# The first batch's filter stage in pairs of PSUM banks: 1024-column products and copies, three products on GpSimd, and one input piece on GpSimd's queue

## The chip, the cores and the metric

The kernel runs on one core of one Trainium2 chip. The metric is device time in microseconds (us); lower is better. The kernel before takes 880.41 us, the median of three runs (879.73 to 880.63).

## The reference

Eight sequences of 3008 rows and 256 columns are filtered along the sequence in the frequency domain, and every row of the result then passes through a gated feed-forward layer. Cut to what matters:

```python
X = np.fft.rfft(x, axis=1)                       # x: (8, 3008, 256)
Y = X * (filt_r + 1j * filt_i)[None, :, :]       # filter: (1505, 256)
y = np.fft.irfft(Y, n=3008, axis=1)
t = y.reshape(8 * 3008, 256)
out = (np.maximum(t @ w_gate, 0.0) * (t @ w_val)) @ w_out   # w: (256,1536), (256,1536), (1536,256)
```

## The kernel before

**The work.** A sequence of 3008 = 94 x 32 rows is transformed in two steps. Step A is a 94-point transform as a matmul with the float32 weights `WA`; for batches 0 and 1 it is `a_bank`, 512 columns a time, and every such item shows in the profile as two passes of TensorE (PE). Step B takes 32 points: `fwd(b, i)` makes eight small matmuls into PSUM tiles `psX`, `product` multiplies them by the real (`Ftr`) and the imaginary (`Fti`) filter into `tt` and `uu`, and `inv(b, i)` transforms both back into `psD`, which is copied to SBUF. Each batch has six groups i. Step C (`item_c`, PSUM tile `psY`) is the last transform and gives the rows `yT` of one block of 512; `gv` and `o_part` are the feed-forward layer on 47 such blocks (`psV`, `psG`, `psO`).

**The order.** All order is written out by hand; each engine runs its instructions in the order in which the program issues them, and waits on semaphores. Batch 0 goes first and alone ("first B", the function `first_b`): step A of batch 0 (`a_0`), the transposes `turn_0` on VectorE (DVE), then the six groups of step B. In between stand small things in the hook `amid(i)`: tables for the way back (`make_back_u`), dummy matmuls on a junk tile (`warm`), and items `a_1` of step A of batch 1. After first B the DVE transposes batch 0 once more (`turn_d`), PE works off the rest of the `a_1` items, and the first `item_c` follows; it needs `turn_d`. From there on the feed-forward blocks run without a pause, and steps A and B of batches 1 to 7 are strewn in between them.

**PSUM.** There are eight banks of 512 float32 columns; `bank()` takes the one that has been free longest, and `done()` gives it back. Each `psX`, `psD`, `psA` of first B is one bank.

**First B before.** A group has two `psX` banks (e = 0, 1), so there are 24 products of 512 columns. The list `POOL_U` gives eight of the `uu` products to GpSimd (POOL): ScalarE (ACT) copies `psX` to an SBUF tile `xs` (L427), and POOL multiplies it (L428). The other sixteen run on DVE from PSUM (L430). Group i's products are followed by `inv(0, i-2)`, whose two `psD` banks are copied by ACT (L455), once by DVE.

**Queues.** The filters arrive on POOL's DMA queue; one half of the partitions is then filled from the other by `place_filter` on SP's queue (L256, SBUF to SBUF, `Fti<-Fti`). The first piece of batch 1's input x goes out on SP's queue between those copies (`load_x`, L192), and the rest behind them.

Of the kernel before, what the change touches and what calls it, by code (L numbers as in the profile page):

```python
# [12 lines left out]
FP32 = mybir.dt.float32  # L13
BF16 = mybir.dt.bfloat16
ALU = mybir.AluOpType
# [16 lines left out]
NG = 24  # L32
# [87 lines left out]
def kernel(  # L120
# [10 lines left out]
    nc = tc.nc  # L131
    B, S_, D = x.shape
# [3 lines left out]
    NC2 = 8  # L136
# [9 lines left out]
    consts = ctx.enter_context(tc.tile_pool(name="consts", bufs=1))  # L146
    dram = ctx.enter_context(tc.tile_pool(name="dram", bufs=1, space=bass.MemoryType.DRAM))
    sb = ctx.enter_context(tc.tile_pool(name="sb", bufs=2))
    ps = ctx.enter_context(tc.tile_pool(name="ps", bufs=1, space=bass.MemoryType.PSUM))
    free, held = list(range(8)), {}  # L150

    def bank(name, *shape):

        i = free.pop(0)
        t = ps.tile([128, *shape], FP32, tag=f"bank{i}", bufs=1, name=name)
        held[id(t)] = i, t
        return t

    def done(t):
        free.append(held.pop(id(t))[0])  # L160

    prologue = ExitStack()
    pro = prologue.enter_context(tc.tile_pool(name="pro", bufs=1))

    Abuf = [dram.tile([NROW * N2, D if b > 1 else D // 2], BF16, name=f"Abuf{b}") if b else None for b in range(B)]
    Dbuf = [dram.tile([NROW * N2, D], BF16, name=f"Dbuf{b}") if b else None for b in range(B)]
# [34 lines left out]

    def make_back_t(q):

        psI = [bank("psI", 4, 64) for _ in range(2)]
        for e in range(2):
            for a in range(2):
                for j in range(4):
                    nc.tensor.matmul(psI[e][64 * a:64 * a + 64, j],
                                     F2[64 * e:64 * e + 64, 12 * a + 4 * q + j, :],
                                     perm[64 * e:64 * e + 64], start=True, stop=True,  # L210
                                     tile_position=(64 * e, 64 * a))
        for e in range(2):
            nc.scalar.copy(I2t[:, 8 * q + e:8 * q + 8:2, :], psI[e])
            done(psI[e])

    def make_back_u(q):

        psI = bank("psI", 8, 64)
        nc.tensor.matmul(psI, swap, I2t[:, 8 * q:8 * q + 8, :], start=True, stop=True)
        nc.scalar.copy(I2u[:, 8 * q:8 * q + 8, :], psI)  # L220
        done(psI)

    def place_own():

# [26 lines left out]
    def place_filter(fi, a, half, copy):  # L251

        dst = FILT[fi][1]
        gs = slice(H * half, H * half + H)
        r = a * 64
        copy(dst[r + 32:r + 64, gs, :], dst[r:r + 32, gs, :])  # L256
# [19 lines left out]
        nc.gpsimd.tensor_copy(scr[:tile_.shape[0]], tile_)  # L276


    def a_bank(n2, nn, d0, nd):

        psA = bank("psA", nn, nd)
        xf = XF[n2 // NX2].rearrange("p (n d) -> p n d", d=D)
        n = n2 % NX2
        nc.tensor.matmul(psA, WA, xf[:, n:n + nn, d0:d0 + nd], start=True, stop=True)  # L284
        return psA

    def a_0(n2, nn, d0, nd):

        psA = a_bank(n2, nn, d0, nd)
        dq = D // 4  # L290
        l, q = n2 % NC2, slice(d0 // dq, (d0 + nd) // dq)
        dst = AS0.rearrange("p q (l c) d -> p l c q d", c=N2 // NC2)[:, l:l + nn, n2 // NC2, q, :]
        nc.scalar.copy(dst, psA.rearrange("p n (q d) -> p n q d", d=dq))
        done(psA)

    def a_1(p, s, h):

        psA = a_bank(NC2 * p + 4 * s, 4, h * D // 2, D // 2)
        if h and len(AS1) == 1:
            for _ in range(2):  # L300
                t = sb.tile([128, NC2 * D], BF16, tag="asb", bufs=3, name="asb")
                AS1.append(t.rearrange("p (l c d) -> p l c d", l=NC2, c=N2 // NC2))
        ts = AS1[1:] if h else AS1[:1]
        w = D // 2 // len(ts)
        for i, t in enumerate(ts):
            nc.scalar.copy(t[:, 4 * s:4 * s + 4, p, :], psA[:, :, i * w:(i + 1) * w])
        done(psA)

    def turn_a(dst, src):
# [86 lines left out]
                              _ap(Abuf[b], (48 * (rr % 2) + 24 * (rr // 2)) * N2 * D,  # L396
                                  [[D, 32], [N2 * D, 24], [1, D]]))

    POOL_U = ((0, 1), (1, 0), (1, 1), (2, 0), (2, 1), (3, 1), (4, 0), (5, 0))
    ats = {}  # L400

    psXs, tus, dsbs, left = {}, {}, {}, {}
# [13 lines left out]
                                     ats[b][64 * e:64 * e + 64, j, :] if b > 1 else ats[b][64 * e:64 * e + 64, :, j, :],  # L416
                                     start=True, stop=True, tile_position=(64 * e, 64 * a))

    def product(b, i, e, k, pool=False):

        psX = psXs[b, i, e]
        pool_, bufs = (fs, 4) if b else (pro, 6)
        p = pool_.tile([128, 2, D], BF16, tag=("tt", "uu")[k], bufs=bufs, name=("tt", "uu")[k])
        filt = (Ftr, Fti)[k][:, 4 * i + e:4 * i + 4:2, :]
        if pool:
            xs = pro.tile([128, 2, D], FP32, tag="xs", bufs=3)
            nc.scalar.copy(xs, psX)  # L427
            nc.gpsimd.tensor_tensor(p, xs, filt, op=ALU.mult)  # L428
        else:
            nc.vector.tensor_tensor(p, psX, filt, op=ALU.mult)  # L430
        tus[b, i, e, k] = p
        left[b, i, e] -= 1
        if not left[b, i, e]:
            done(psX)

    def inv(b, i):

        if b and i in CUTS:
            dsbs[b] = i, sb.tile([128, 2, 4, D], BF16, tag="dsb", bufs=3, name="dsb")
        psD = [bank("psD", 2, D) for a in range(2)]  # L440
        for m in range(2):
            for k in range(2):
                for a in range(2):
                    for e in range(2):
                        nc.tensor.matmul(psD[a][64 * e:64 * e + 64, m],  # L445
                                         (I2t, I2u)[k][64 * a:64 * a + 64, 4 * i + 2 * m + e, :],
                                         tus[b, i, e, k][64 * a:64 * a + 64, m],
                                         start=(k == 0), stop=(k == 1),
                                         tile_position=(64 * a, 64 * e))
        if b:  # L450
            i0, dsb = dsbs[b]
            o = 2 * (i - i0)
        for a in range(2):
            copy = nc.vector.tensor_copy if (b, i, a) == (0, 5, 0) else nc.scalar.copy
            copy(dsb[:, a, o:o + 2, :] if b else DS0[:, 12 * a + 2 * i:12 * a + 2 * i + 2, :], psD[a])  # L455
            done(psD[a])
        if b and i + 1 in CUTS:
            for q in range(4):
                nc.sync.dma_start(_ap(Dbuf[b], (64 * (q // 2) + q % 2) * NG * D + 2 * i0 * D,
                                      [[2 * NG * D, 32], [NG // 2 * D, 2], [1, (o + 2) * D]]),  # L460
                                  dsb[32 * q:32 * q + 32, :, :o + 2, :])

    def first_b(amid):

        for i in range(6):
            fwd(0, i)
            on_pool = [(i, e) in POOL_U for e in range(2)]
            seq = {(0, 0): ((0, 0), (0, 1), (1, 0), (1, 1)), (0, 1): ((1, 1), (0, 0), (0, 1), (1, 0)),
                   (1, 0): ((0, 1), (1, 0), (1, 1), (0, 0)), (1, 1): ((0, 0), (1, 1), (0, 1), (1, 0))}
            for e, k in seq[tuple(map(int, on_pool))]:  # L470
                product(0, i, e, k, pool=k == 1 and on_pool[e])
            if i > 1:
                inv(0, i - 2)
            amid(i)
        inv(0, 4)
        amid(6)
        inv(0, 5)

    dCs = {(0, z): dCb[:, 8 * z:8 * z + 8, :] for z in range(NZ)}

# [96 lines left out]

    def warm(n, cols=512):

        psJ = bank("psJ", 512)  # L580
        for i in range(n):
            nc.tensor.matmul(psJ[:, :cols], junk[:, 0:128], junk[:, :cols], start=True, stop=True)
        done(psJ)

    q = NX2 * D // 4
    both, sp = (nc.sync, nc.scalar), (nc.sync,)
# [19 lines left out]

    warm(18, 256)
    new_at(0)
    for n2, h in ((0, 0), (0, 1), (4, 0), (4, 1)):
        a_0(n2, 4, h * D // 2, D // 2)  # L610
    for i, (p, dq) in enumerate(((1, 0), (1, 1), (2, 0), (2, 1), (3, 0), (3, 1), (1, 2), (2, 2), (3, 2),
                                 (1, 3), (2, 3), (3, 3))):
        a_0(NC2 * p, NC2, dq * D // 4, D // 4)
        if p == 3:
            turn_0(dq)
        if i > 9:
            make_back_t(i - 10)
    make_back_t(2)
    for i in range(3):
        warm(2)  # L620
    place_filter(1, 0, 0, nc.gpsimd.tensor_copy)
    for fi, a, half in ((0, 0, 0), (0, 1, 0), (1, 1, 0), (0, 0, 1), (0, 1, 1)):
        place_filter(fi, a, half, nc.sync.dma_start)
    load_x(1, sp, ((0, 0, 2 * q),))
    for a in range(2):
        place_filter(1, a, 1, nc.sync.dma_start)
    load_x(1, sp, ((0, 2 * q, 4 * q), (1, 0, 2 * q), (1, 2 * q, 4 * q)))
    items = iter([(p, s, h) for p, h in ((0, 0), (1, 0), (2, 0), (0, 1), (3, 0), (1, 1), (2, 1), (3, 1))
                  for s in range(2)])

    def amid(i):
        if i < 3:
            make_back_u(i)
            warm(3)
        else:
            a_1(*next(items))
        if i == 3:
            place_nyq()
            place_own()

    first_b(amid)
    load_vg(0, DFF // 2)
    load_vg(DFF // 2, DFF)
    load_o()
# [92 lines left out]
```

## Time and profile before

| | |
|---|---|
| Median of the runs | 880.41 us (879.73 to 880.63) |
| The profiled execution | 880.49 us, with a span of 878.4 us |
| Busy in the span | PE 99%, DVE 66%, ACT 57%, POOL 41% |
| Transfers | 102.85 MB, 117 GB/s in the mean |

The profile is one execution. "Span" runs from the first to the last instruction; 2.09 us of the time lie outside it. Times within it are counted from its start. In the lists by time, a row gives start, duration, engine, line of the code, operation, output and inputs, how many instructions were merged, and in brackets the idle time before them with what ended it. PEld are the weight loads of TensorE, which run beside its matmuls.

### The profile page before, as it was taken

To read this page: it belongs to the slowest core of one execution; us is meant where nothing else is said; L and a number is where in the kernel's file an instruction comes from. 1 tells how busy PE (TensorE), PEld (TensorE's weight loads), DVE (VectorE), ACT (ScalarE), POOL (GpSimd) and SP (SyncE) were. 2 spreads that over 40 slices of the span, in tenths; PEclk is the share of its full clock that TensorE was granted. 3 is DMA by queue.
4 is the path that set the end of the run, shared out by engine and by line. 5 is a ranking of instruction groups with operands and counts; after the bars stand their busy time and mean duration, and the time that the engine had idled before them with its cause. 6 is when DMAs were issued, how large, how long until landed. Compare 5 with 4: busy or idle time off the path is not lost.

```text
span 878.4 us, 19202 instructions
## 1 busy us (share of the span) xinstructions
PE 868.5 (99%) x7184; PEld 507.4 (58%) x7184; DVE 576.5 (66%) x863; ACT 500.7 (57%) x905; POOL 364.3 (41%) x367
## 2 busy tenths in 40 slices
PE   8899999999999999999999999999999999999998
PEld 3445655666555665556655665556655656666665
DVE  4787766667666776567665777657766577655553
ACT  4865655565555656555655565555565555555553
POOL 7718940166901688017870287603884000000001
PEclk9999999999999999999999999999999999999999
DMA  9996454634754347634475344663445512421111
GB/s 251 239 179 110 133 140 106 128 93 102 187 120 101 105 109 181 132 92 101 119 190 114 83 117 126 166 126 88 124 134 141 119 40 69 98 60 36 38 32 53
DMA packets 107075, 102.85 MB, mean 117 GB/s; under 512 B 24216, under 2 KB 92344, under 8 KB 106215
## 3 DMA queue, kind: packets, MB, share of 16 engines
q1 hardware_dynamic: 83974, 74.45, 34.7%
q0 software_dynamic: 22608, 26.41, 13.0%
q8 instruction: 56, 0.92, 0.5%
q10 hardware_dynamic: 400, 0.79, 0.3%
q14 instruction: 37, 0.29, 0.1%
HBM read 58.16 MB, written 45.88 MB: 118 GB/s over the span
## 4 chain that ended last, share of the span: by engine, by line
PE 95%; DMA 3%; POOL 1%; DVE 1%; ACT 0%; issue 0%; SPq 0%; DVEq 0%; POOLq 0%
PE psV L526 29%; PE psG L526 28%; PE psO L547 27%; PE psF L377 3%; PE psY L509 2%; PE psD L445 2%; PE psX L414 2%; PE psA L284 2%; DMA Fti<-Fti 1%; DMA XF<-in_x_dram 1%; DMA Fti<-in_filt_i_dram 1%; POOL out_dram L571 0%; DMA out_dram<-XF 0%; DVE uu L430 0%; DVE prod L531 0%
## 5 line engine op out<-in xcount | busy, mean ns | idle before, releaser
L531 DVE SCALAR_TENSOR_TENSOR prod<-psG,vsb 128x512 bf16<-128x512 f32 x564 | 388.4, 689 | 256.2 <-ACT vsb L529 250.1
L529 ACT CAST vsb<-psV 128x512 bf16<-128x512 f32 x564 | 331.9, 589 | 262.8 <-PE psV L526 171.1
L526 PE MATMUL psV<-yT,WvT 128*128 128x512 bf16 x1128 | 336.7, 379 | 0.6 <-DVE yT L517 0.6
L547 PE MATMUL psO<-WoT,prod 128*128 128x256 bf16 x2256 | 336.5, 273 | 0.0
L526 PE MATMUL psG<-yT,WgT 128*128 128x512 bf16 x1128 | 335.3, 379 | 0.0
L547 PEld LDWEIGHTS <-prod 128*128 128x128 bf16 x2256 | 220.7, 98 | 143.4
L526 PEld LDWEIGHTS <-WgT 128*128 128x128 bf16 x1128 | 110.0, 98 | 134.5 <-issue 1.5
L276 POOL CAST scr<-prod 128x8 f32<-128x8 bf16 x24 | 4.5, 189 | 284.5 <-DVE prod L531 284.5
L526 PEld LDWEIGHTS <-WvT 128*128 128x128 bf16 x1128 | 98.3, 98 | 41.4 <-issue 30.2
L571 POOL DMA_DIRECT2D out_dram<-osb x5 | 2.7, 535 | 200.1 <-ACT osb L560 200.0
L560 ACT COPY osb<-psO 128x512 f32<-128x512 f32 x92 | 53.9, 586 | 25.9 <-PE psO L547 23.8
L430 DVE TENSOR_TENSOR tt<-psX,Ftr 128x512 bf16<-128x512 f32 x96 | 64.8, 680 | 0.9 <-PE psX L414 0.5
L430 DVE TENSOR_TENSOR uu<-psX,Fti 128x512 bf16<-128x512 f32 x88 | 59.8, 680 | 1.9 <-DMA Fti<-Fti 1.9
L363 POOL TENSOR_TENSOR fold<-XF 128x1024 f32<-128x1024 f32 x24 | 57.6, 2401 | 3.7 <-DMA XF<-in_x_dram 3.0
L350 POOL DMA_DIRECT2D XF<-in_x_dram x96 | 56.7, 596 | 3.7 <-PE psY L509 1.5
L364 POOL TENSOR_TENSOR XF<-XF 128x1024 f32<-128x1024 f32 x24 | 56.4, 2350 | 1.9
L455 ACT CAST dsb<-psD 128x512 bf16<-128x512 f32 x84 | 45.1, 589 | 11.0 <-PE psD L445 11.0
L384 DVE CAST asb<-psF 128x512 bf16<-128x512 f32 x48 | 30.9, 686 | 17.8 <-PE psF L377 17.8
L384 ACT CAST asb<-psF 128x512 bf16<-128x512 f32 x48 | 25.8, 589 | 29.0 <-PE psF L377 29.0
L515 ACT CAST yT<-psY 128x512 bf16<-128x512 f32 x47 | 27.5, 586 | 23.1 <-PE psY L509 23.0
L509 PE MATMUL psY<-M,dCb 96*128 96x94 bf16 (+19 forms) x604 | 37.5, 198 | 0.0
L509 PEld LDWEIGHTS <-dCb 96*128 96x128 bf16 (+1 forms) x604 | 34.5, 97 | 3.3 <-issue 0.8
(69 smaller groups left out, 472.2 us busy)
## 6 DMA issues: line engine op xcount, KB each, us to landing
XF<-in_x_dram POOLq DMA_DIRECT2D x48, 256.0 KB, 6.2
Dbuf<-dsb SPq DMA_DIRECT2D x84, 128.0 KB
dCb<-Dbuf SPq DMA_DIRECT2D x56, 192.0 KB
XF<-in_x_dram POOLq DMA_DIRECT2D x96, 96.0 KB, 2.7
Abuf<-asb SPq DMA_DIRECT2D x96, 96.0 KB
at<-Abuf SPq DMA_DIRECT2D x24, 384.0 KB
out_dram<-osb SPq DMA_DIRECT2D x69, 94.0 KB
XF<-in_x_dram SPq DMA_DIRECT2D x20, 256.0 KB
```

Of the source, the lines that this page charges most:

```text
L350: nc.gpsimd.dma_start(xp[r:r + 24, 0:4:2, :], _ap(x, (b * N1 * N2 + o) * D, [[N2 * D, 24], [47 * N2 * D, 2], [1, 512]]))
L363: tt(t, xp[:, 0:2], xp[:, 2:4], op=ALU.add)
L364: tt(xp[:, 2:4], xp[:, 0:2], xp[:, 2:4], op=ALU.subtract)
L384: copy(asf[:, :, q, :], banks[q])
L430: nc.vector.tensor_tensor(p, psX, filt, op=ALU.mult)
L455: copy(dsb[:, a, o:o + 2, :] if b else DS0[:, 12 * a + 2 * i:12 * a + 2 * i + 2, :], psD[a])
L509: nc.tensor.matmul(psY[:, o:o + w], dCs[b, n2 // 8][:, n2 % 8, h * 128:(h + 1) * 128], M1[:, 1, n1:n1 + w] if b == 0 else M1[:NROW, 0, n1: ...
L526: nc.tensor.matmul(pt[:, :W], w[:, h, ft * 128:(ft + 1) * 128], yt[:, h, :], start=(h == 0), stop=(h == 1))
L529: nc.scalar.copy(vsb, psV[:, :W])
L531: nc.vector.scalar_tensor_tensor(prod, in0=psG[:, :W], scalar=0.0, in1=vsb, op0=ALU.max, op1=ALU.mult)
L547: nc.tensor.matmul(psO[:, t % 2], prods[ft][:, t * 128:(t + 1) * 128], WoT[:, ft, :], start=(ft == 0), stop=(ft == NFT - 1))
L560: copy(osb[:, t0 % 2:t % 2 + 1], psO[:, t0 % 2:t % 2 + 1])
```

## The change

First B uses four pairs of banks from a pool of its own, `ps0`, with fixed parts: pairs 0 and 1 are `psX`, pair 2 is `psD`, pair 3 is `psA` of batch 1 and the junk. A product, an `xs` copy and a `psD` copy then cover 1024 columns in one instruction. `POOL_U` goes: POOL has the `uu` product of groups 1, 2 and 4. The three `make_back_u` stand ahead of first B, and `place_own` ahead of it too; of the 512-column junk matmuls, six stand ahead of first B as before, and four instead of three in each of the groups 0, 1 and 2. `amid` of groups 3, 4 and 5 has two `a_1` items each, with one pair and one set of copies; before, groups 3, 4, 5 and one more call had one each. The first x piece of batch 1 goes out on POOL's queue, and the last two filter copies on SP's queue move up ahead of the other pieces. After first B the pool is closed and the eight single banks are used as before.

```diff
+    def pair(i, name):
+        return ps0.tile([128, 2, 512], FP32, tag=f"pair{i}", bufs=1, name=name)
...
     def make_back_t(q):
-        psI = [bank("psI", 4, 64) for _ in range(2)]
+        psI = pair(3, "psI").rearrange("p e (j n) -> p e j n", n=64)
...
-        for e in range(2):
-            nc.scalar.copy(I2t[:, 8 * q + e:8 * q + 8:2, :], psI[e])
-            done(psI[e])
+        nc.scalar.copy(I2t[:, 8 * q:8 * q + 8, :].rearrange("p (j e) n -> p e j n", e=2), psI[:, :, 0:4])
...
+    def a_1_pair(p, h):
+        psA = pair(3, "psA")
+        for s in range(2):
+            a_mm(psA[:, s], NC2 * p + 4 * s, 4, h * D // 2, D // 2)
+        out_1(psA.rearrange("p s (l d) -> p (s l) d", d=D // 2), p, 0, NC2, h)
...
+    def first_fwd(i):
+        psX = pair(i % 2, "psX").rearrange("p e (m d) -> p e m d", m=2)
...
+    def first_product(i, k, psX, pool):
+        p = pro.tile([128, 2, 2, D], BF16, tag=("tt", "uu")[k], bufs=3, name=("tt", "uu")[k])
+        filt = FILT[k][1][:, 4 * i:4 * i + 4, :].rearrange("p (m e) d -> p e m d", e=2)
+        if pool:
+            xs = pro.tile([128, 2, 2, D], FP32, tag="xs", bufs=2, name="xs")
+            nc.scalar.copy(xs, psX)
+            nc.gpsimd.tensor_tensor(p, xs, filt, op=ALU.mult)
+        else:
+            nc.vector.tensor_tensor(p, psX, filt, op=ALU.mult)
...
+    def first_inv(i):
+        psD = pair(2, "psD").rearrange("p a (m d) -> p a m d", m=2)
+        inv_mm([psD[:, a] for a in range(2)], 0, i)
+        dst = DS0[:, 0:NG, :].rearrange("p (a o) d -> p a o d", a=2)[:, :, 2 * i:2 * i + 2, :]
+        if i < 5:
+            nc.scalar.copy(dst, psD)
+        else:
+            nc.vector.tensor_copy(dst[:, 0], psD[:, 0])
+            nc.scalar.copy(dst[:, 1], psD[:, 1])
...
         for i in range(6):
-            fwd(0, i)
...
+            psX = first_fwd(i)
+            pool = i in (1, 2, 4)
+            for k in (1, 0) if pool else (0, 1):
+                first_product(i, k, psX, pool and k == 1)
             if i > 1:
-                inv(0, i - 2)
+                first_inv(i - 2)
             amid(i)
-        inv(0, 4)
-        amid(6)
-        inv(0, 5)
+        first_inv(4)
+        first_inv(5)
...
     for i in range(3):
-        warm(2)
+        make_back_u(i)
+    warm(6)
     place_filter(1, 0, 0, nc.gpsimd.tensor_copy)
-    for fi, a, half in ((0, 0, 0), (0, 1, 0), (1, 1, 0), (0, 0, 1), (0, 1, 1)):
+    for fi, a, half in ((0, 0, 0), (0, 1, 0), (1, 1, 0), (0, 0, 1), (0, 1, 1), (1, 0, 1), (1, 1, 1)):
         place_filter(fi, a, half, nc.sync.dma_start)
-    load_x(1, sp, ((0, 0, 2 * q),))
-    for a in range(2):
-        place_filter(1, a, 1, nc.sync.dma_start)
+    load_x(1, (nc.gpsimd,), ((0, 0, 2 * q),))
     load_x(1, sp, ((0, 2 * q, 4 * q), (1, 0, 2 * q), (1, 2 * q, 4 * q)))
+    place_own()
...
         if i < 3:
-            make_back_u(i)
-            warm(3)
+            warm(4)
         else:
-            a_1(*next(items))
-        if i == 3:
+            a_1_pair(*((0, 0), (0, 1), (1, 0))[i - 3])
+        if i == 2:
             place_nyq()
-            place_own()
 
     first_b(amid)
+    front.close()
+    ps = ctx.enter_context(tc.tile_pool(name="ps", bufs=1, space=bass.MemoryType.PSUM))
+    items = [(p, s, h) for p, h in ((2, 0), (3, 0), (1, 1), (2, 1), (3, 1)) for s in range(2)]
```

In the built program, before and after hold the same instructions from the first `item_c` on; the order on each engine differs only ahead of it. Of `a_1` items, two-pass each, nine are left between the last `inv` and the first `item_c` after the change, and eleven before it.

## The prediction

> **What bounds the kernel now.** I read the busy time by stretches first, to see in which part time can be won at all.
>
> ```profile
> 0.00:40.00 40.00, 34.93 (x270) 15.82 (x271) 22.63 (x26) 25.63 (x49) 30.04 (x45) 1.00 0.92 251
> 50.00:860.00 810.00, 809.35 (x6779) 477.10 (x6778) 539.18 (x824) 462.33 (x828) 328.07 (x312) 1.00 0.46 111
> ```
>
> The first pair of numbers is the stretch and its length, the next is PE's busy time. From 50 us on PE stands still for 0.65 us of 810: that part is work, and the change doesn't touch it. So the whole question is when the first feed-forward matmul (`psV`) starts; what comes behind it moves along one for one. The chain of waits, in order of time (start, duration, what), shows what sets that moment:
>
> ```profile
> 28.09 4.53 DMA Fti<-Fti
> ...
> 32.74 0.70 DVE uu L430
> ...
> 37.61 1.06 PE psA L284 x2
> 38.66 0.56 PE psD L445 x16
> 39.23 9.64 PE psA L284 x22
> 48.86 0.47 PE psY L509 x12
> 49.33 0.95 PE psA L284 x2
> 50.28 0.43 PE psV L526 x2
> ```
>
> The last filter copy lands at 32.65 and holds up a `uu`; then DVE and PE pass the work on closely, and from 39.2 PE runs eleven `a_1` items (x22 passes, 9.64 / 11 = 0.87 each) up to `psY`. `turn_d` is hidden there. The instructions by time:
>
> ```profile
> 36.21 1.09 ACT L455 CAST AS<-psD 128x512 bf16<-128x512 f32 x2
> 37.54 1.13 PE L284 MATMUL psA<-XF,WA 128*128 128x512 f32 x2
> 40.06 7.35 DVE L311 STREAM_TRANSPOSE dCb<-AS 128x2048 f32<-128x2048 f32 x2
> 49.37 0.69 DVE L517 CAST yT<-psY 128x512 bf16<-128x512 f32 x1 [1.96 <-PE psY L509]
> 50.12 0.59 PE L526 MATMUL psV<-yT,WvT 128*128 128x512 bf16 x2
> ```
>
> `turn_d` ends at 47.41, 1.3 us before `psY`. `psV` starts at 50.12: the number to beat. Prices come from the groups by shape (count, then busy and mean ns):
>
> ```profile
> L455 ACT CAST AS<-psD 128x512 bf16<-128x512 f32 x11 | 6.2, 630 | 0.1
> L306 ACT CAST asb<-psA 128x256 bf16<-128x256 f32 x14 | 4.5, 375 | 1.6 <-PE psA L284 1.6
> L428 POOL TENSOR_TENSOR uu<-xs,Fti 128x512 bf16<-128x512 f32 x8 | 9.1, 1153 | 3.3 <-ACT xs L427 2.3 <-DMA Fti<-Fti 0.8
> L430 DVE TENSOR_TENSOR uu<-psX,Fti 128x512 bf16<-128x512 f32 x4 | 2.7, 682 | 1.9 <-DMA Fti<-Fti 1.9
> ```
>
> **Prices of the wide forms** (estimates; no row shows them). ACT undisturbed takes 0.58 for 512 columns and 0.375 for 256, so 0.8 ns a column and 0.99 for 1024; in a row each takes 0.10 less. Its ends are 0.90 and twice 0.58 = 1.16; I take the slope. DVE follows the next every 0.60; at 1024 I take 1.13 (duration 1.21; ends 1.18 and 1.36). POOL's `fold` takes 1.27 at 512 and 2.41 at 1024, so 1.155 becomes 2.25.
>
> **What is shed.** DVE: sixteen products x 0.60 = 9.6 become nine x 1.13 = 10.2, so nothing is won. POOL: 9.2 become 6.8. ACT: eight `xs` and eleven `psD` copies x 0.48 = 9.1 become three and five x 0.89 and one x 0.58 = 7.7. Two `a_1` items, 1.7, move from behind first B into it. The last two filter copies on SP's queue no longer wait behind three x issues (24.47 to 27.26): they go out at about 25.4 and 26.0 instead of 27.36 and 28.09, and at 4.5 land by 30.6. DVE's 1.89 stall on them goes. But what is late next is another thing, below.
>
> **POOL's queue.** It now issues three x pieces (0.5 to 0.6 each) between 23.87 and 25.6 and the two `place_own` copies (0.29 each) by 26.3. POOL was idle there until 26.22 and now gets its first `xs` at 28.5: nothing is queued behind it in need, and it costs nothing. `uu` of group 2 ends at 33.0, `inv(2)` wants it at 33.8; `uu` of 4 ends at 37.7, `inv(4)` comes at 39.7. The weight loads behind it go out at 37.7, as before (37.61).
>
> **What is added: hand-overs.** Before, eight banks rotate, so PE may run ahead of the copies. After, `psD` is one pair and `psA` one pair, so each `inv` waits for the copy of the last one, and each `a_1` pair for its own predecessor's; PE is in order, so `fwd` of the next group is queued behind. The waits in the built program say the same: each `psD` and `psA` group waits for ACT. I lay this out step by step, an instruction starting when its engine is free and its inputs are there, 0.05 for a hand-over. The same reckoning on the kernel before gives 50.07 for `psV`, against 50.12 measured.
>
> - The tables: `make_back_t` has one pair, so each of the three waits for a copy (0.58). Third copy 23.67 to 24.25, third `make_back_u` at 24.30, then six junk matmuls x 0.216. `fwd(0)` starts at 25.81; before, it started at 25.01 when the transpose was done.
> - `tt(0)` 26.30, `uu(0)` 27.43 to 28.64. `fwd(2)` needs pair 0: 28.69. `xs(2)` 29.18 to 30.17, behind it on ACT the copy of `psD(0)`, to 31.06.
> - `inv(1)` 31.11; `a_1` pair: 0.20 for its weights and 4 x 0.43, 31.55 to 33.52; copy (0.99) to 34.56.
> - Second pair 34.61 to 36.58; two copies of 512 (1.06) to 37.69. Third pair 37.74 to 39.72; copy to 40.76. In between ACT copies `psD`; behind the third it is `psD(4)`, to 41.64.
> - `inv(5)` 41.69 to 42.33. Its DVE half to 43.06, and the ACT half waits for DVE in the built program (before, both ran at once, 39.26 and 39.30): to 43.69. Closing the pool makes the first single-bank `a_1` wait for that copy.
> - Nine `a_1` items: 0.20 + 9 x 0.857 = 7.9, 43.74 to 51.65. `turn_d` (7.35) runs 43.74 to 51.08 and stays hidden by 0.6. `psY` 51.65, 0.43, the last `a_1` 1.06, `psV` at 53.14.
>
> DVE, freed from the filter, stands idle for `xs(4)` until 35.50 instead: 1.9, as long as the stall that went. Sum: 53.14 - 50.07 = 3.07 later. In other words: PE reaches the single `a_1` items at 38.96 in the same reckoning before and at 43.74 after, 4.78 later, and the two items already done give back 1.71. On this execution's 880.49 (span 878.4 and 2.09 around it) that is 883.56; the median is 0.08 lower, so 883.5. Five wide ACT copies and two wide products lie on this chain: their ends give -0.5 and +1.15.
>
> **A clock that could drop.** After, between 40.3 and 43.7 PE is busy for about 0.5 us; before, the thinnest such stretch, 22.0 to 25.4, has 2.30 busy of 3.4, and the passes behind it keep their 0.43. So no row shows what so little work does. That there is a slower pace the start shows: eighteen 256-column matmuls in 4.02 us, 0.22 each, the time that 512 columns take later, while the granted clock reads 1.00 there too. The Trainium skill, "TensorE: Matmul & The Clock Gate", speaks against the change here: its section "A second HAM failure mode: psum-queue depth-cycling" tells of a PE that idles a little at every round of its banks and swings between half and full rate, and "What's actually happening" puts the idle window at about 3.4 us. By the first, the single `a_1` items would start slowly; by the second, two gaps of 1.6 us each stay below the limit unless they count as one.
>
> **The rivals.**
> - *Half pace from 43.7.* The start ran slowly from 1.1 to at least 4.95 and at full pace by 7.87, so for some 5 us. The same again, with the nine items on it, does 2.5 us of work in 5: 883.5 + 2.5 = 886.0. For it: the thin stretch; against it: neither gap is over 1.6, and one of 1.1 before left no trace.
> - *The x piece lands late.* POOL's 256 KB loads took 10.2 us in the median in the first 80 us; the third, issued at 25.1, would land at 35.3, and the first `a_1` pair, due at 31.55, holds PE for 3.8: 887.3. Against it: that median is from loads of 2 KB runs in a crowd; here the rows are 8 KB, and 0.8 MB at the 250 GB/s of this stretch need 3 us.
> - *Faster: DVE, not the hand-overs, sets first B.* From 26.3 nine products x 1.13 and the two waits for `xs` of 0.5 end at 37.5, `inv(5)` at 38.0, the split copy and `turn_d` at 46.8, `psV` at 48.3: 878.7 or a little less. For it: this bounds it before, after 32.7. It needs the chain from `inv(1)` to the first single `a_1` (31.1 to 43.7, 12.6) to take under 9.5 to break even; its four `a_1` and copy steps alone are 9.1, so almost no wait could be left.
> - *Partly so*: hand-overs and copies shorter than priced by over 1.4 in all: within the bound, about 881.5.
>
> That the change doesn't do what it says is out: the built program has the 1024-column products, three on POOL, and the filter copies ahead.
>
> **How the numbers follow.** A measurement of this kernel can tell about 0.2% (1.8 us, 878.6 to 882.2) from no change. Chances: 0.66 for the forecast (slower), 0.10 for half pace and 0.08 for the late x piece (both slower), 0.10 for the partial case (same), 0.06 for the faster rival. Slower 0.84, same 0.10, faster 0.06. The range goes from 881.6, the partial case, to 886.2, the half-pace case; the late piece and the faster rival are left out.
>
> **What would show it.** Right: `fwd(0)` near 25.8; no wait for `Fti<-Fti` on DVE, but 1 to 2 us for `xs`; `a_1` pairs each waiting for an ACT copy; a PE gap of 1.6 before `inv(5)` and one before the first single `a_1`; `psV` near 53.1; after it the same 0.65 us of stalls. Wrong: `psV` before 51.5, or `psX` and `psD` groups that wait for DVE alone; passes of `psA` at over 0.5 (half pace); PE waiting for XF (x late); 1024-column copies that aren't near 0.99.

## The result, and the profile after

The changed kernel takes 885.58 us in the median of four runs (884.99 to 886.98), the kernel before beside it 880.52 (four runs): 1.0061 times the time, interval 1.0043 to 1.0078. It is slower by 5.06; the forecast was 883.5, slower by 3.07. The profiled run took 886.10, with a span of 884.1.

The chain of waits of the changed kernel, in order of time (start, duration, what), cut to first B's hand-overs:

```profile
32.34 0.63 PE psD L444 x16
32.97 1.93 PE psA L284 x4
...
34.92 1.02 ACT dCb L304
...
35.98 2.00 PE psA L284 x4
...
38.00 1.08 ACT asb L304 x2
...
39.13 2.00 PE psA L284 x4
...
41.15 1.01 ACT dCb L304
42.16 0.92 ACT AS L498
...
43.13 0.66 PE psD L444 x16
...
43.80 0.70 DVE AS L500
...
44.53 0.59 ACT AS L501
...
45.17 9.69 PE psA L284 x18
54.86 0.47 PE psY L546 x12
```

Before, the chain from 37.61 on was PE alone; now PE and ACT take turns, one pair at a time, as forecast. But the last step but one has a size that nobody put down for it: nine items as x18 passes take 9.69, and before, eleven items as x22 passes took 9.64. The rows by time of the same trace (in brackets the idle time before the row, and what ended it):

```profile
36.88 1.22 DVE L488 TENSOR_TENSOR tt<-psX,Ftr 128x1024 bf16<-128x1024 f32 x1 [1.99 <-ACT xs L485]
43.13 0.30 PE L444 MATMUL psD<-tt,I2t 64*64 64x256 bf16 x4 [1.45 <-ACT AS L498]
45.15 7.26 DVE L321 STREAM_TRANSPOSE dCb<-AS 128x2048 f32<-128x2048 f32 x2 [0.65 <-ACT AS L501]
45.17 9.69 PE L284 MATMUL psA<-XF,WA 128*128 128x512 f32 x18 [1.41 <-ACT AS L501]
56.11 0.59 PE L563 MATMUL psV<-yT,WvT 128*128 128x512 bf16 x2
```

The two gaps of the forecast, 1.45 ahead of `inv(5)` and 1.41 ahead of the first single `a_1`, are there, and DVE waits for `xs` rather than for the filter. `psV` comes at 56.11 instead of 50.12. What the 9.69 is shows in the busy time by stretches (stretch, length, busy PE, PEld, DVE, ACT and POOL with counts, then the granted clock, the DMA share and GB/s):

```profile
41.80:45.20 3.40, 0.66 (x17) 0.39 (x16) 0.74 (x2) 1.86 (x3) 2.19 (x4) 1.00 1.14 195
45.86:49.27 3.41, 3.41 (x6) 1.36 (x5) 3.41 (x2) 1.17 (x2) 0.00 (x0) 0.50 1.15 204
49.27:52.68 3.41, 3.41 (x9) 1.49 (x9) 3.14 (x1) 2.18 (x6) 0.00 (x0) 1.00 1.44 196
```

Between 41.8 and 45.2 PE is busy for 0.66 of 3.40; soon after, its granted clock halves. The trace records when the clock changes: to half at 45.86 and back at 49.27, 3.41 later. At half pace that loses 1.70, and at full pace the same x18 take 7.96 to 7.99 (below). The Trainium skill, "TensorE: Matmul & The Clock Gate", section "What's actually happening", speaks of a free-running window of some 3.4 us; the 3.41 agrees with it, and no gap here is near that long by itself.

Starts within an execution move by about a microsecond with the first loads, so traces are compared from the start of the last `a_0` item (20.96 before, 22.07 after) to `psV`: 29.16 before, 34.04 after. The times of the two profiled runs differ by 5.61: 4.88 in this distance, 1.11 ahead of it, and -0.38 behind (880.49 - 50.12 = 830.37 before, 886.10 - 56.11 = 829.99 after). The last `a_0` of eleven further profiles started anywhere from 19.69 to 22.69, so the 1.11 of one pair of profiles is no finding. Behind `psV` nothing has moved.

### The profile page after: what moved, and what is told of

Read it like the earlier page. It is cut to its first block, busy times and chain, and to the rows that moved or that the text cites. A ratio compares the mean times of both kernels' runs of the same rounds, so it can differ in the third digit from the quotient of the medians.

```text
span 884.1 us, 19047 instructions
## 1 busy us (share of the span) xinstructions
PE 863.4 (98%) x7066; PEld 508.3 (57%) x7187; DVE 577.5 (65%) x856; ACT 499.2 (56%) x888; POOL 363.2 (41%) x365
## 4 chain that ended last, share of the span: by engine, by line
PE 93%; ACT 2%; DVE 2%; issue 1%; DMA 1%; POOL 0%; DVEq 0%
PE psG L563 28%; PE psO L584 27%; PE psV L563 26%; PE psA L284 3%; PE psF L387 3%; PE psD L444 2%; PE psY L546 2%; PE psX L423 2%; DVE prod L568 2%; ACT vsb L566 1%; DMA XF<-in_x_dram 1%; POOL out_dram L608 0%; ACT dCb L304 0%; ACT AS L498 0%; DMA out_dram<-XF 0%
## 5 line engine op out<-in xcount | busy, mean ns | idle before, releaser
L563 PE MATMUL psG<-yT,WgT 128*128 128x512 bf16 x1107 | 330.8, 379 | 5.1
L563 PE MATMUL psV<-yT,WvT 128*128 128x512 bf16 x1030 | 315.5, 380 | 0.9 <-DVE yT L554 0.6
L432 DVE TENSOR_TENSOR tt<-psX,Ftr 128x512 bf16<-128x512 f32 x84 | 57.2, 681 | 0.0
L432 DVE TENSOR_TENSOR uu<-psX,Fti 128x512 bf16<-128x512 f32 x84 | 57.2, 681 | 0.0
L284 PE MATMUL psA<-XF,WA 128*128 128x512 f32 x64 | 31.5, 634 | 5.5 <-issue 1.7
```

Source lines behind the costliest of these rows:

```text
L432: nc.vector.tensor_tensor(p, psX, FILT[k][1][:, 4 * i + e:4 * i + 4:2, :], op=ALU.mult)
L563: nc.tensor.matmul(pt[:, :W], w[:, h, ft * 128:(ft + 1) * 128], yt[:, h, :], start=(h == 0), stop=(h == 1))
```

## The experiments

Two theories were set against each other: the hand-overs of single pairs make all of the loss, or they make some 3.2 and the halved clock the rest. A third question was what the queues do.

**Fill the gaps (fill).** Junk matmuls in the two gaps, into the pair that `a_1` uses:

```diff
         first_inv(4)
+        warm(4)
         first_inv(5)
+        warm(6)
```

> The changed kernel with four junk matmuls between the last two inv and six behind the last one, in PE's two gaps of 1.4 us; nothing waits for their result. Theory (hand-overs cost 3.1, and the thin stretch from 41.7 to 45.2 halves PE's clock for 3.4 us, 1.7 lost): the granted clock stays 1.00 between 40 and 50 us, the 18 passes of the single a_1 items take 7.8 instead of 9.69, and the time falls by 1.7 to about 883.9, still 3.2 above the kernel before. Rival (the passes are slow because transfers or turn_d run beside them): they stay near 9.7, and the time near 885.6.

Measured: 884.10 (five runs), the kernel before 880.36 in the same comparison, ratio 1.0044 (1.0027 to 1.0062). In its profile the clock stayed at 1.00 between 40 and 50 us and the x18 took 7.96, with `turn_d` and the transfers still beside them, so these are not what slows the passes. One of the five runs (887.51) has a mean clock of 0.998. But another wait had come in, the first `a_1` pair on its input:

```profile
31.91 1.52 PE L284 MATMUL psA<-XF,WA 128*128 128x512 f32 x3 [0.94 <-DMA XF<-in_x_dram]
```

This execution's front had come 2.0 earlier (last `a_0` at 20.08). The x pieces on POOL's queue had gone out only 0.94 earlier (23.26 instead of 24.20), and their median time to landing was 6.9 instead of 5.8. So the run was repeated with the queues as before the change.

**The queues put back (undoq), and both (fillq).** undoq is the change without its queue part; fillq is fill and undoq together.

```diff
-    for fi, a, half in (..., (1, 0, 1), (1, 1, 1)):
+    for fi, a, half in (...):
         place_filter(fi, a, half, nc.sync.dma_start)
-    load_x(1, (nc.gpsimd,), ((0, 0, 2 * q),))
+    load_x(1, sp, ((0, 0, 2 * q),))
+    for a in range(2):
+        place_filter(1, a, 1, nc.sync.dma_start)
```

> The changed kernel with the queue part undone: the first x piece on SP's queue between the filter copies, as before. Theory: the pairs' chain runs beside either order, so the time stays within 0.7 of the changed kernel; the Fti copy lands near 32.7 and uu of group 3 waits some tenths for it. Rival (the x piece on POOL's queue holds PE): 1 or more faster.

> The changed kernel with the junk matmuls in PE's two gaps, as before, and with the first x piece back on SP's queue, since with those matmuls alone PE then waited 0.9 for that piece. Theory (hand-overs 3.1, clock 1.7): from the start of the last a_0 item to the first psV 32.3, where the changed kernel has 34.0 and the kernel before 29.2; clock 1.00 in nearly all runs; time 1.7 below the changed kernel, about 3.3 above the kernel before. Rival (the clock has no part; 34.0 is the hand-overs' own): 34.0 and 5 above.

Measured: undoq 886.29 (884.39 to 886.67, four runs), a second look at the changed kernel beside it 885.09; distance 34.03 in both. The queues are worth nothing inside the change: DVE waits 0.31 for the filter copy again, and 1.58 instead of 1.99 for `xs`. fillq took 884.66 (five runs) against 880.14: 1.0049 (1.0037 to 1.0062). Its rows by time and by stretches:

```profile
44.95 7.96 PE L284 MATMUL psA<-XF,WA 128*128 128x512 f32 x18
54.16 0.59 PE L565 MATMUL psV<-yT,WvT 128*128 128x512 bf16 x2
```

```profile
40.00:50.00 10.00, 9.36 (x56) 4.00 (x55) 6.27 (x4) 5.34 (x9) 3.59 (x6) 1.00 1.12 175
```

The distance is 32.44 as expected: with every hand-over still in place, 1.60 of the 4.88 is gone, and on this path only the junk and, with it, the clock differ from undoq. By distance fillq should lie 3.28 above the kernel before; its median lies 4.5 above. That 1.2 is not explained: behind `psV` its profiled run has 831.17, 0.8 more than before, but other profiles scatter there from 829.86 to 831.66.

**The same kernel again (after_again).**

> The changed kernel itself, beside the others on one chip, since runs of one kernel scatter by about 1 us. Both theories: about 885.5, 5 above the kernel before; in the profile the granted clock falls to about half for some 3 us behind the last inv.

Measured: 885.09 (884.06 to 888.24, six runs), ratio 1.0057 (1.0040 to 1.0074). Of the ten runs of the changed kernel in the two comparisons, nine have a mean clock of 0.995 to 0.998 and one has 1.000 (884.65). Half pace for 3.4 of 884 us is a mean of 0.998, so the drop seems frequent but not certain. The mean also counts a half pace at the end of the kernel, where PE has nothing left to do (in fill's profile from 879.59 on). A mean of 0.998 comes in the kernel before too (7 of 60 runs, none lower), so a single such run of another kernel proves nothing; half of the changed kernel's ten runs lie lower.

**All products on DVE (alldve).** The three wide products of POOL and their copies go.

```diff
-            pool = i in (1, 2, 4)
+            pool = False
```

> The changed kernel with all twelve products on DVE, none on POOL, and no xs copies. Theory (PE and ACT hand-overs set the stage, not POOL or DVE): DVE takes 3.4 more and ACT 2.7 less, both beside the chain; the time stays within 1 of the changed kernel. Rival (three of twelve on POOL is what costs, through xs copies ahead of psD copies on ACT): 1.5 or more faster. Rival (DVE is the bound): 2 or more slower.

Measured: 886.28 (884.88 to 886.51, four runs), ratio 1.0062 (1.0046 to 1.0078). Its profiled execution (884.88, clock 1.000) is the case that the forecast had in mind, since it has both gaps and no drop:

```profile
42.73 0.30 PE L444 MATMUL psD<-tt,I2t 64*64 64x256 bf16 x4 [1.46 <-ACT AS L498]
44.77 7.99 PE L284 MATMUL psA<-XF,WA 128*128 128x512 f32 x18 [1.41 <-ACT AS L501]
54.01 0.59 PE L563 MATMUL psV<-yT,WvT 128*128 128x512 bf16 x2
```

```profile
41.40:44.80 3.40, 0.66 (x17) 0.39 (x16) 0.74 (x2) 1.86 (x3) 0.00 (x0) 1.00 1.19 205
```

A stretch with the same 0.66 busy of 3.40 ended without a drop here; its other three runs have clocks of 0.995 to 0.998 and took 1.2 to 1.6 more. So the hand-overs alone make a distance of 32.38, 3.22 more than before, and POOL's share of the products is worth nothing either way: the same distance came out of fillq with three products on POOL.

**Single banks for `a_1` in first B (asplit); the last `inv` into the free `psX` pairs (inv5).** asplit replaces pair 3 by two banks with a copy of each; inv5 takes `psD` of the last group from pairs 0 and 1 and copies both halves on DVE.

```diff
-        psA = pair(3, "psA")
         for s in range(2):
-            a_mm(psA[:, s], ...)
-        out_1(psA..., p, 0, NC2, h)
+            psA = hbank(s, "psA")
+            out_1(a_mm(psA, ...), p, 4 * s, 4, h)
```

```diff
+        if i == 5:
+            psDs = [pair(a, "psD")[:, 0]... for a in range(2)]
...
-            nc.scalar.copy(dst[:, 1], psD[:, 1])
+            nc.vector.tensor_copy(dst[:, 1], psDs[1])
```

> The changed kernel with psA of first B in two single banks instead of one pair, and a 512-column copy behind each item (the tables' psI and the junk use the same two banks). Theory (the hand-over at the one psA pair is on the path): the first copy runs beside the second item, so each of the three a_1 steps gets about 0.5 shorter; the first psV comes 1.6 earlier, at about 54.5 where the profile of the changed kernel has 56.1, and the time falls to about 884.0, with the clock drop still there. Rival (x or filter transfers hold the stage): no change, 885.6.

> The changed kernel with the last inv writing to the two psX pairs, which are free by then, instead of waiting for psD, and both of its copies on DVE. Theory: the gap of 1.45 ahead of the last inv goes, the copies take 1.3 instead of 1.37, and turn_d and the single a_1 items start 1.6 earlier: 884.0 if the clock still drops, about 882.3 if it doesn't, since only one thin gap is left. Rival (the stage ends with what DVE or the transfers allow): no change, 885.6.

Measured, each against 880.36: asplit 883.32 (ten runs, 1.0025, 1.0014 to 1.0036), inv5 883.05 (ten runs, 1.0026, 1.0011 to 1.0042). Rows by time of asplit, then of inv5:

```profile
41.77 0.30 PE L447 MATMUL psD<-tt,I2t 64*64 64x256 bf16 x4 [1.11 <-ACT AS L501]
43.81 7.99 PE L288 MATMUL psA<-XF,WA 128*128 128x512 f32 x18 [1.41 <-ACT AS L504]
```

```profile
43.51 7.96 PE L284 MATMUL psA<-XF,WA 128*128 128x512 f32 x18 [1.43 <-ACT AS L502]
```

asplit's distance is 31.53 and holds 0.55 of waiting for the x piece; without that 30.98, so the waits of the `a_1` pairs were 1.4 of the 3.22. inv5's is 30.68: its gap ahead of `inv(5)` is gone, which is 1.7 of the 3.22, and the gap of 1.43 that the closing of the pool makes remains. In both profiles the clock stayed at 1.00, where asplit's expectation had the drop. The thinnest 3.40 us of first B's end have 0.87 us of PE work in asplit and 1.97 in inv5. Three of asplit's ten runs and two of inv5's have a mean clock of 0.998 or less, and they are the slowest of each.

**Both, and the pool kept open (best1), with four junk matmuls fewer (best2).** The single `a_1` items run on pairs 2, 0 and 1 of `ps0`, and the pool is closed ahead of the first `item_c`. shortwarm is the changed kernel with the last edit alone.

```diff
     first_b(amid)
-    front.close()
-    ps = ctx.enter_context(tc.tile_pool(name="ps", ...))
...
         if (p, s, h) == (3, 0, 1):
+            front.close()
+            ps = ctx.enter_context(tc.tile_pool(name="ps", ...))
```

```diff
-    warm(6)
+    warm(2)
```

> The changed kernel, still with 1024-column products and psD copies, but without its hand-overs: psA of first B in two single banks with a copy each, the last inv on the freed psX pairs with both copies on DVE, and the nine single a_1 items on banks of the same pool, so that they needn't wait for its closing. Theory (hand-overs and the clock that drops in their gaps are the whole loss): psV comes 2.8 earlier than in the reckoning for the changed kernel, at about the same distance from the last a_0 item as in the kernel before (29.2) and not 34.0; clock 1.00; time about 880.8. Rival (a rest of the loss lies in the wide instructions, in POOL's share or in the queue): 882.5 or more.

> The version without hand-overs (two single psA banks, last inv on the psX pairs, single a_1 items on the open pool) with two junk matmuls instead of six ahead of first B. Theory: 0.86 off its 29.8, so 29.0 from the last a_0 item to psV, level with the 29.2 of the kernel before; time 880.4 to 881.0. If the wide instructions were worth anything by themselves: below 880.

> The changed kernel with two junk matmuls instead of six behind the make_back_u. Theory (they are on the path, as the tables hold PE until 24.5 in the reckoning and the transpose ends at 25.0): fwd of group 0 starts 0.86 earlier, and so does psV if the clock does the same as in the changed kernel: 33.2 from the last a_0 item instead of 34.0; time about 884.7. Rival (the later chain swallows it): 34.0, and 885.5.

Measured: best1 881.72 (twelve runs) against 880.56, 1.0013 (1.0005 to 1.0022); best2 881.35 (eleven runs) against 880.14, 1.0013 (1.0004 to 1.0021); shortwarm 885.69 (four runs), 1.0064 (1.0049 to 1.0080). best1's rows by time:

```profile
42.35 7.99 PE L288 MATMUL psA<-XF,WA 128*128 128x512 f32 x18 [0.68 <-ACT AS L511]
51.12 0.62 PE L559 MATMUL psY<-M,dCb 128*128 128x94 bf16 x12 [0.78 <-ACT asb L308]
52.53 0.59 PE L576 MATMUL psV<-yT,WvT 128*128 128x512 bf16 x2
```

The distance falls to 29.84, 0.68 above before, and the wait for the closing of the pool now stands ahead of `psY` (0.78). The parts do not add up: asplit's 1.4 and inv5's 1.7 are 3.1, while best1, which has both edits and this new wait, is 2.54 below alldve's 32.38. In twelve runs the mean clock was never under 0.999; the thinnest 3.40 us ahead of its nine items have 2.72 us of work. Giving the pairs their freedom back undoes the loss but for about 1 us in the medians (best1 was expected at 880.8): no version here beats the kernel before. best2's distance is 29.73 where 29.0 was expected, since PE waits 0.53 for the x piece, and its time misses the expected 880.4 to 881.0. shortwarm's expectation, 33.2, was missed: PE then waits 0.70 for the x piece, and the distance is 33.91.

**The queue part alone on the kernel before (qalone).** The filter copies ahead, the x piece on POOL's queue.

> The kernel before with only the queue part of the change: the first x piece of batch 1 on POOL's queue, the last two filter copies ahead of the other x pieces on SP's. No pairs. Theory (the queue part is harmless and frees DVE from the wait for the filter copy, 1.9 us, of which the rest of the stage gives back 0.7): psV comes 1.2 earlier than 50.12 and the time is about 879.3. Rival (the x piece on POOL's queue is what made the change slow): 881.5 or more, with POOL or PE waiting for XF.

Measured: 880.66 (eleven runs) against 880.36, 0.9999 (0.9987 to 1.0010): no difference, where a gain was expected. The chain of waits, and DVE's row by time:

```profile
24.35 1.04 POOL XF L192 x2
25.39 6.93 DMA XF<-in_x_dram
...
32.45 1.10 PE psA L284 x2
```

```profile
32.89 0.69 DVE L430 TENSOR_TENSOR uu<-psX,Fti 128x512 bf16<-128x512 f32 x1 [0.89 <-DMA Fti<-Fti]
```

DVE's wait for the filter falls from 1.9 to 0.89 rather than to nothing, and the x piece takes 6.93 by POOL's queue and lands at 32.32; PE waits 0.38 for it. The distance in this profile is 28.18, 0.98 less than before; its time is not less. As with fillq, the microsecond between the two was not found.

## Why the prediction was right and wrong

**Right: the direction and its mechanism.** PE loses the rotation of eight banks and waits for each copy. By the reckoning `psV` moves by 3.07; with the hand-overs in place and a steady clock it moved by 3.22 (alldve) and 3.28 (fillq). Step by step, alldve's trace less the 0.67 by which its last `a_0` is later: first single `a_1` at 44.10 (forecast 43.74), its nine items up to `psY` 7.83 (7.91), `psV` at 53.34 (53.14). `fwd(0)` of the changed kernel started at 27.02, less 1.11 is 25.91 (25.81). "`turn_d` stays hidden by 0.6": it ends at 52.01 in alldve, 0.59 before `psY`; under the slow clock it has 2.3.

**Right: the trade on DVE.** The stall on the filter copy went and one of 1.99 for `xs` took its place (1.9). That neither filter copies nor POOL's products would be worth anything is what undoq and alldve show.

**Wrong: the likeliest case took the clock as steady.** The step that failed is the weighing of the thin stretch: half pace was a rival with a chance of 0.10, since neither gap was long and one of 1.1 before left no trace. It came: passes of `psA` at over 0.5, the prediction's own sign for it, stand in the profiles of four runs, and nine of the changed kernel's ten runs have a low mean clock. The rival's place was right; its price, 2.5 from the slow start of the kernel, was too high, since the pace stays halved for 3.41 and not for 5: 1.70. (That the clock column reads 1.00 in the slow start says nothing: the trace of the kernel before records no clock ahead of 5.67, where it goes up.) Forecast of the hand-overs and measured drop together give 883.5 + 1.7 = 885.2, against 885.58. That 885.58 lies inside the stated range is partly luck: the upper end, 886.2, comes from the half-pace case at 2.5, and with 1.7 it would have been about 885.4.

The argument counted gaps one by one; what the drop follows is how much PE does in one window of a fixed grid. The thinnest 3.40 us hold 0.63 us of work in each of the four profiles with a drop (the changed kernel twice, undoq, shortwarm), and 0.63 in alldve's, which has none, so the stretch alone does not decide. But in each profile all recorded changes of the granted clock lie a whole number of steps of 3.413 us apart; in the changed kernel's they are up at 4.89, down at 45.86, twelve steps later, and up at 49.27. The busy time in the grid's windows is, for the last window ahead of the drop in the changed kernel, after_again, undoq and shortwarm, and then for the two windows that share the thin stretch in alldve:

```profile
42.44:45.85 3.41, 1.31 (x18) 0.80 (x18) 1.39 (x2) 1.22 (x2) 1.55 (x3) 1.00 1.14 193
40.68:44.09 3.41, 0.67 (x17) 0.40 (x16) 0.75 (x2) 1.87 (x3) 2.20 (x4) 1.00 1.10 187
40.73:44.14 3.41, 1.11 (x17) 0.66 (x17) 1.19 (x2) 1.42 (x2) 1.71 (x3) 1.00 1.11 185
39.99:43.41 3.42, 1.38 (x18) 0.85 (x18) 1.46 (x2) 1.17 (x2) 1.49 (x3) 1.00 1.15 195
39.44:42.85 3.41, 1.96 (x24) 0.79 (x27) 1.28 (x2) 2.08 (x3) 0.00 (x0) 1.00 1.15 207
42.85:46.27 3.42, 2.01 (x20) 1.02 (x16) 2.21 (x2) 0.92 (x2) 0.00 (x0) 1.00 1.31 201
```

The four windows with 0.67 to 1.38 us of PE work are each followed by one at half pace. In alldve a line of the grid at 42.85 cuts the thin stretch in two, each window keeps about 2 us, and no drop follows. best1 shows the same earlier on: a stretch of 0.75 in 3.40 (12.90 to 16.30, while PE waits for x) is cut at 14.91 into windows of 2.09 and 2.08, and the clock stays. In all 13 profiles together, from the first recorded change on, the 17 windows that are followed by half pace (13 of them at the end of a kernel) hold 1.40 us or less, and all the more than 3300 others 1.46 or more. So what decided in these profiles is how the stretch lay on the grid. How often it happens stays open: in the changed kernel's trace about half of all positions of the grid would put 1.4 us or less into one window, which is less than nine runs of ten.

The Trainium skill, "TensorE: Matmul & The Clock Gate", section "A second HAM failure mode: psum-queue depth-cycling", tells of short PE idles at every turn of the banks that swing the clock; this trace agrees, with one swing.

**Partly wrong: POOL's queue "costs nothing".** In the changed kernel's profile the x piece came just in time (the first `a_1` at 32.90 shows no wait for it). In five of the other profiles PE waited 0.38 to 0.94 for it (fill, asplit, qalone, shortwarm, best2); in four with the same queue it did not (after_again, inv5, alldve, best1). The start of the last `a_0` does not sort them: it waited at 22.11 (qalone) and not at 20.96 (after_again). The late x piece was a rival at 3.8; its measured size is below 1.

**Prices.** The groups by shape of the changed kernel (count, then busy and mean ns):

```profile
L498 ACT CAST AS<-psD 128x1024 bf16<-128x1024 f32 x5 | 5.1, 1021 | 0.7 <-PE psD L444 0.7
L488 DVE TENSOR_TENSOR uu<-psX,Fti 128x1024 bf16<-128x1024 f32 x3 | 3.6, 1215 | 0.0
L486 POOL TENSOR_TENSOR uu<-xs,Fti 128x1024 bf16<-128x1024 f32 x3 | 6.4, 2127 | 4.8 <-issue 4.8
```

ACT's wide copy takes 1.02 (forecast 0.99), DVE's product 1.215 (1.21), POOL's 2.13 (2.25). None of them moved the result. The rivals of DVE as the bound and of shorter hand-overs are out: no `inv` or `a_1` pair waits for DVE, and the gaps are 1.45 and 1.41 where 1.6 was forecast. (The "four `a_1` and copy steps" in that rival's argument are three, 3.01 + 3.08 + 3.02 = 9.1.)

## What to carry to other kernels

Wider instructions save little where they are paid by the column, and they take buffers out of rotation: count how many banks each stage has left, and lay out who waits for whose copy, before counting instructions. When PE and another engine begin to take turns, add up PE's work over a few microseconds, not gap by gap; if it is very thin, price a stretch at half pace as part of the forecast. Here that meant 1.4 us or less of work in one 3.41 us window. The price is a chance and not a certainty, since the grid lies differently in each execution: its first recorded line came anywhere from 4.12 to 6.59 us after the span's start. A stall that goes from one engine is worth something only if the next input on that path is early as well, as the two microseconds that DVE first lost to the filter and then to `xs` show.

## What the runs showed that was not expected

- After a stretch with 0.63 us of PE work in 3.40, made of gaps no longer than 1.46, the granted clock halved for 3.41 us in each of the four profiles that show it (the changed kernel twice, undoq, shortwarm). The drop came 0.03 to 0.75 after the first single `a_1` had started, so the whole loss fell on busy PE.
- The same stretch does not always bring it: alldve's profile keeps 1.00 between 40 and 50 us, with a line of the grid inside the stretch, and one of ten runs of the changed kernel has a mean of 1.000.
- A 256 KB load on POOL's queue took 6.93 from the end of its issue to landing (qalone), and up to 7.6 in asplit; the median of such loads in the changed kernel is 5.8.
- About 1 us between kernels (fillq, qalone) appears in the medians and not in the distances. With one profile each it stays open.
